# A Fourier-mixing and squared-ReLU kernel: the first phase and the first block in another order

## The chip, the cores and the metric

The kernel runs on one core of a Trainium2 chip. Its time is the device time of one execution in microseconds (us). The engines are TensorE (PE, matrix products; PEld is its weight load), VectorE (DVE), ScalarE (ACT), GpSimd (POOL), and SyncE (SP), whose queue here issues nearly all transfers.

## The reference

For x of 8 x 3008 x 256 the reference takes a Fourier transform along the sequence and one along the features, keeps the real part, and runs a two-layer network with a squared ReLU over all 24064 rows:

```python
def _attn_ref(x):
    X = np.fft.fft(x, axis=1)
    X = np.fft.fft(X, axis=2)
    return X.real.astype(np.float32)

def _moe_ref(x, w_in, w_out):        # w_in 256 x 2048, w_out 2048 x 256
    h = x @ w_in
    r = np.maximum(h, 0.0)
    g = r * r
    return (g @ w_out).astype(np.float32)
```

## The kernel before

**What is computed where.** The transform over the features is merged into the first weights: `G1` is the cosine matrix times `w_in`, `G2` the sine matrix times `w_in` (127 rows), and `gE` holds half the alternating sum of each column of `w_in`. The transform over the sequence is made once per batch from folded input: `Pt` (cosine part, 128 features), `Qt` (sine part, 127 features) and `Et` (feature 128, repeated over the partitions), each with 1505 columns, the rows of the sequence up to its middle. The rest follows by mirror symmetry: a product with `Pt` and one with `Qt`, once added and once subtracted, give the rows on both sides.

**The weights arrive as 64-bit floats** and are turned into 32-bit ones on the chip by `convert` (L213 on): a raw tile is fetched by two transfers (L227); VectorE cuts out exponent (L234) and mantissa (L239); ScalarE does three operations (L236, L237, L241); `finish` then does three on VectorE (L244, L246, L247). Raw tiles take turns in four buffers, three of which are also the buffers of x. `load_win(j)` converts one eighth of `w_in` and returns `finish` and `products`, which computes this eighth of `G1`, `G2` (L262, copied by ScalarE at L263) and `gE` (L268, L270). `load_wout(j)` converts one eighth of `w_out`.

**First phase (first batch, L711 to L747).** x comes in seven tiles (384 to 512 KB each). Tiles 0 to 3 hold the even rows of the folded sequence, tiles 4 to 6 (from `ODD0`) the odd ones. `for_p(t)` folds a tile for the cosine part (L356, L372, L386), `for_q(t)` for the sine part (L360, L376, L386). Thirty `groups` then make `Pt` (0 to 9), `Et` (10 to 19) and `Qt` (20 to 29), five for each parity of the output: products over tiles 0 to 3 (`even_n`), two joins, products over tiles 4 to 6 (`odd_n`), the last join (`join_1`, L468 to L472), which writes `Pt`, `Et` or `Qt`. The tables `cosT` and `sinT` are loaded by 13 transfers each (L182): ten small ones for tiles 0 to 3 and three large ones for tiles 4 to 6. All of x is issued ahead of both tables; the first eighth of `w_in` ahead of all.

**Main loop (L767).** A batch has six blocks of about 251 columns and each block eight steps `j`. In a step, `front` multiplies 2 x 128 columns of the hidden layer (PE L551 and L552), and VectorE forms the sums (L554, L556, L557); `combine` squares on ScalarE (L566, L567) and, outside the first block, prepares sums on POOL for a scheme with seven products instead of eight; `back`, two steps later, multiplies by `w_out`: L591 in the first block, L604 elsewhere. In the first block (steps 0 to 7) the other eighths of the weights are converted and multiplied between `back` and the next `front` (L796 to L798). In the second block `sum_wout` forms combinations of `w_out` (L282 to L285). Folding and transform of the next batch are "side work": `between`, called twice a step, takes pieces from a list by their estimated times. For the second batch it starts in the second block at half pace.

**What sets the order.** Nothing is rescheduled: each engine carries out its instructions in the order in which the code issues them. The PSUM buffers are: two for `front` (psh, tag h), two for the transform and `gE` (psd, tag d), and four accumulators mA to mD (psm). The order of issue is therefore the schedule, and a wait on one engine holds everything behind it on this engine.

The lines of the first phase and of the loop that the change replaces are printed here.

Of the kernel before, what the change touches and what calls it, by code (L numbers as in the profile page):

```python
# [13 lines left out]
P = 128  # L14
# [67 lines left out]
def kernel(  # L82
# [78 lines left out]
    sind = const.tile([P, 2, P - 1], F32, name="sind")  # L161
    altd = const.tile([P, 2, 1], F32, name="altd")
# [6 lines left out]
    G2 = const.tile([P - 1, F], F32, name="G2")  # L169
    gE = const.tile([P, NFC], F32, name="gE")  # L170

    def load_table(tab, src, engine):

        for t, (c, r0, step, rows) in enumerate(TILES):
            for i, (s0, count) in enumerate(row_tiles(S)):
                mine = [r for r in range(count) if (s0 + r - r0) % step == 0 and 0 <= (s0 + r - r0) // step < rows]
                if mine:
                    o, m = (s0 + mine[0] - r0) // step, len(mine)
                    while m % 15 and m % 16 and o + m < P and mine[0] + step * m < P:
                        m += 1  # L180
                    nk = NC[0][c]
                    engine.dma_start(out=tab[o:o + m, :, PLACE[t]:PLACE[t] + nk],  # L182
                                     in_=src[mine[0]:mine[0] + step * (m - 1) + 1:step, :, i, 0:nk])
# [5 lines left out]
    for dst, src in ((cosd, cos_d), (sind, sin_d), (altd, alt_d)):  # L189
        nc.scalar.dma_start(out=dst, in_=src.rearrange("(c p) m -> p c m", p=P))  # L190

# [61 lines left out]
    def load_win(j):  # L253
# [4 lines left out]
        def products():  # L258
            for tab, G, n in ((cosd, G1, P), (sind, G2, P - 1)):
                ps = psh.tile([P, CH], F32, name="pg", tag="h")  # L260
                for i in range(2):
                    nc.tensor.matmul(ps[0:n], tab[:, i], w[:, i], start=i == 0, stop=i == 1)  # L262
                nc.scalar.copy(G.rearrange("p (h j f) -> j p h f", h=2, j=NJ)[j],  # L263
                               ps[0:n].rearrange("p (h f) -> p h f", h=2))
            ps = psd.tile([P, CH], F32, name="pe", tag="d")
            for h in range(2):
                for i in range(2):
                    nc.tensor.matmul(ps[:, h:h + 1], w[:, i, h * P:(h + 1) * P], altd[:, i],  # L268
                                     start=i == 0, stop=i == 1)
            nc.scalar.mul(gE[:, j::NJ], ps[:, 0:2], 0.5)  # L270

        return finish, products

    def load_wout(j):

        return convert(wout[:, j].rearrange("p h c e -> p h (c e)"), pair_out(j)), lambda: None
# [158 lines left out]
    def dft_ops(b):  # L435
# [7 lines left out]
        def group(kp, which):  # L443
# [40 lines left out]
            def odd_n():  # L484
                ps = psd.tile([P, 512], F32, name="pd", tag="d")[0:n]
# [55 lines left out]
    def front(b, k0, n, j, between):  # L541
# [4 lines left out]
        for h in range(2):  # L546
# [5 lines left out]
            nc.tensor.matmul(hQ, G2[:, fs], qt[:, ks], start=True, stop=True)  # L552
# [29 lines left out]
    def back(n, j, g, s, final):  # L582

        if j == 0:
            for nm in ("mA", "mB", "mC", "mD"):
                acc[nm] = psm.tile([P, 2, CH], F32, name=nm, tag=nm)
# [20 lines left out]
    def gather(n, plain, final):  # L607


        mA, mB, mC, mD = (acc[nm] for nm in ("mA", "mB", "mC", "mD"))  # L610
        if plain:
# [3 lines left out]
            return c  # L615
        sA = ep.tile([P, 2, CK], F32, name="sA", tag="sA")
# [64 lines left out]


    weights = [lambda j=j: load_win(j) for j in range(2)]
    for j in range(NJ):
        weights.append(lambda j=j: load_wout(j))
        if j + 2 < NJ:
            weights.append(lambda j=j: load_win(j + 2))

    def next_weight():

        nonlocal begun
        (finish, products), begun = begun, weights.pop(0)() if weights else None
        finish()
        return products

# [15 lines left out]
    begun = weights.pop(0)()  # L711
    for t in range(NT):
        load_x(0, t)
    load_table(cosT, cos_s, nc.sync)
    load_table(sinT, sin_s, nc.sync)
    start()
    for_p(0)
    finish, products = begun
    finish()
    products()  # L720
    for t in range(1, 4):
        for_p(t)
    groups_at(0, 5)
    for_p(4)
    for_q(0)
    for_q(1)
    groups_at(1, 2)
    for_p(5)
    groups_at(6, 7)
    for_p(6)  # L730
    groups_at(3)
    for_q(4)
    groups_at(4, 8)
    for_q(5)
    groups_at(9, 10)
    for_q(6)
    groups_at(11, 12, 13)
    begun = weights.pop(0)()
    groups_at(15)
    for_q(2)  # L740
    groups_at(14, 16, 17, 18)
    for_q(3)
    groups_at(20, 19, 25)
    products = [next_weight()]
    groups_at(21, 22, 23, 26, 27, 28)
    next_weight()
    groups_at(24, 29)  # L747
# [6 lines left out]
    def between():  # L754
# [3 lines left out]
        if i < NJ or i % NJ == LAG - 1:  # L758
            return
        spent -= pace / 2 if i < 2 * NJ else pace  # L760
        while side and spent <= 0:
            t, f = side.pop(0)
            f()
            spent += t

    flight, finished = [], []
    for i in range(len(steps) + LAG + 4):  # L767
        if i < len(steps):
# [8 lines left out]
            if i % per == 0:  # L777
                assert not side
                side = ahead(b + 1) if b + 1 < B else []
                calls = 2 * (NJ - 1) * len(BLOCKS) - 6  # L780
                spent, pace = 0.0, sum(t for t, _ in side) / (calls - (0 if i else 3 * (NJ - 1)))
            g = front(b, k0, n, j, between)
            if i < NJ:
                s = combine(n, g, True)
            elif i < 2 * NJ:
                sum_wout(j)
# [9 lines left out]
        for f in products:  # L796
            f()
        products = [next_weight() for _ in range(2 if 0 < i < NJ - 2 else 1 if i < NJ else 0)]  # L798
# [65 lines left out]
```

## Time and profile before

| what | value |
|---|---|
| median of 3 runs | 1963.36 us (1962.3 to 1965.45) |
| the profiled execution | 1965.78 us, span of its instructions 1964.0 us |
| PE busy | 1929.5 us (98% of the span) |
| PEld, DVE, ACT, POOL busy | 1708.3, 1399.8, 924.9, 1170.2 us |
| chain that ended last | PE 93%, DVE 3%, DMA 1%, ACT 1% |
| mean granted PE clock | 0.992 |

The page cuts the span into 40 slices of 49 us. PE is at 9 tenths in all but the first (5 tenths, granted clock 7 tenths) and the last. In the first slice the DMA engines are busy 6 tenths of the time and move 186 GB/s, later 11 to 55. So the first 100 to 130 us differ from the rest, and answers about single stretches, lines and waits are needed for them. A row of such an answer names a line, an engine, an operation and its tiles; "[0.74 <-ACT ...]" says that the engine was idle for 0.74 us ahead of it and that ACT ended that wait.

### The profile page before, as it was taken

To read this page: it belongs to the slowest core of one execution; us is meant where nothing else is said; L and a number is where in the kernel's file an instruction comes from. 1 tells how busy PE (TensorE), PEld (TensorE's weight loads), DVE (VectorE), ACT (ScalarE), POOL (GpSimd) and SP (SyncE) were. 2 spreads that over 40 slices of the span, in tenths; PEclk is the share of its full clock that TensorE was granted. 3 is DMA by queue.
4 is the path that set the end of the run, shared out by engine and by line. 5 is a ranking of instruction groups with operands and counts; after the bars stand their busy time and mean duration, and the time that the engine had idled before them with its cause. 6 is when DMAs were issued, how large, how long until landed. Compare 5 with 4: busy or idle time off the path is not lost.

```text
span 1964.0 us, 27513 instructions
## 1 busy us (share of the span) xinstructions
PE 1929.5 (98%) x9160; PEld 1708.3 (87%) x9160; DVE 1399.8 (71%) x3434; ACT 924.9 (47%) x1076; POOL 1170.2 (60%) x1705
## 2 busy tenths in 40 slices
PE   5999999999999999999999999999999999999998
PEld 4788888888988889888988889888898888988887
DVE  7889866777677776777667776677767777656554
ACT  1654544445344544444444454444544454444443
POOL 0026745667566765666557765666756676556564
PEclk7999999999999999999999999999999999999999
DMA  6332101210121111111011200121002101100101
GB/s 186 113 50 52 27 13 39 50 27 20 16 51 41 21 29 27 40 30 38 11 35 33 48 19 11 35 54 27 19 15 53 33 11 22 27 11 11 22 11 22
DMA packets 145340, 68.88 MB, mean 35 GB/s; under 512 B 129003, under 2 KB 136110, under 8 KB 145197
## 3 DMA queue, kind: packets, MB, share of 16 engines
q1 hardware_dynamic: 144121, 66.60, 15.4%
q8 instruction: 72, 1.18, 0.2%
q10 hardware_dynamic: 1076, 0.52, 0.1%
q14 instruction: 71, 0.58, 0.1%
HBM read 42.39 MB, written 24.68 MB: 34 GB/s over the span
## 4 chain that ended last, share of the span: by engine, by line
PE 93%; DVE 3%; DMA 1%; ACT 1%; issue 0%; SPq 0%; DVEq 0%; ACTq 0%
PE ph L552 16%; PE ph L551 16%; PE mC L604 16%; PE mA L604 16%; PE mB L604 16%; PE mD L604 8%; PE pd L455 3%; PE pd L500 2%; DMA xt<-in_x_dram 1%; DVE he L554 1%; DMA raw<-in_moe_w_in_dram 1%; DVE g L557 0%; DVE g L556 0%; ACT g L566 0%; ACT g L567 0%; DMA cosT<-in_cos_s_dram 0%
## 5 line engine op out<-in xcount | busy, mean ns | idle before, releaser
L566 ACT ACTIVATE g<-g 128x1004 f32<-128x1004 f32 (+1 forms) x384 | 399.5, 1040 | 818.7 <-DVE g L557 421.3
L574 POOL TENSOR_TENSOR s<-g 128x251 f32<-128x251 f32 (+1 forms) x376 | 246.1, 655 | 718.9 <-ACT g L567 657.5
L554 DVE SCALAR_TENSOR_TENSOR he<-Et,gE,ph 128x251 f32<-128x251 f32 (+1 forms) x768 | 361.8, 471 | 421.5 <-PE ph L552 420.4
L551 PE MATMUL ph<-Pt,G 128*128 128x251 f32 (+1 forms) x1536 | 451.8, 375 | 4.2 <-ACT G L263 3.4
L552 PE MATMUL ph<-Qt,G 127*128 127x251 f32 (+1 forms) x1536 | 451.4, 374 | 0.2 <-DVE Qt L468 0.2
L567 ACT ACTIVATE g<-g 128x1004 f32<-128x1004 f32 (+1 forms) x384 | 399.2, 1040 | 12.2
L604 PE MATMUL mC<-s,wsum 128*128 128x251 f32 (+1 forms) x1504 | 381.4, 374 | 0.0
L604 PE MATMUL mA<-g,wout 128*128 128x251 f32 (+1 forms) x1504 | 379.8, 374 | 0.0
L556 DVE TENSOR_TENSOR g<-he,ph 128x251 f32<-128x251 f32 (+1 forms) x768 | 320.5, 417 | 54.4 <-POOL s L574 0.5
L551 PEld LDWEIGHTS ph<-Pt,G 128*128 128x128 f32 x1536 | 287.2, 189 | 42.2 <-ACT G L263 4.0
L552 PEld LDWEIGHTS ph<-Qt,G 127*128 127x128 f32 x1536 | 291.2, 190 | 36.4 <-DVE Qt L468 0.6
L604 PEld LDWEIGHTS mC<-s,wsum 128*128 128x128 f32 x1504 | 285.5, 190 | 34.6
L557 DVE TENSOR_TENSOR g<-he,ph 128x251 f32<-128x251 f32 (+1 forms) x768 | 314.2, 409 | 0.0
L604 PEld LDWEIGHTS mA<-g,wout 128*128 128x128 f32 x1504 | 282.8, 189 | 34.7 <-issue 0.6
L575 POOL TENSOR_TENSOR s<-s,g 128x251 f32<-128x251 f32 (+1 forms) x376 | 283.3, 754 | 29.5
L576 POOL TENSOR_TENSOR s<-g 128x251 f32<-128x251 f32 (+1 forms) x376 | 295.3, 785 | 0.0
L577 POOL TENSOR_TENSOR s<-g,s 128x251 f32<-128x251 f32 (+1 forms) x376 | 255.1, 678 | 0.0
L604 PE MATMUL mB<-g,wsum 128*128 128x251 f32 (+1 forms) x752 | 220.5, 374 | 0.0
L604 PE MATMUL mD<-s,wout 128*128 128x251 f32 (+1 forms) x752 | 220.3, 374 | 0.0
L604 PE MATMUL mB<-s,wout 128*128 128x251 f32 (+1 forms) x752 | 219.9, 374 | 0.0
L604 PEld LDWEIGHTS mB<-g,wsum 128*128 128x128 f32 x752 | 142.6, 190 | 17.4
L604 PEld LDWEIGHTS mD<-s,wout 128*128 128x128 f32 x752 | 141.9, 189 | 17.7
(118 smaller groups left out, 1292.1 us busy)
## 6 DMA issues: line engine op xcount, KB each, us to landing
out_dram<-os SPq DMA_DIRECT2D x376, 56.0 KB
xt<-in_x_dram SPq DMA_DIRECT2D x32, 384.0 KB
xt<-in_x_dram SPq DMA_DIRECT2D x42, 128.0 KB
Et<-e_dram SPq DMA_DIRECT2D x7, 752.5 KB
xt<-in_x_dram SPq DMA_DIRECT2D x9, 512.0 KB
out_dram<-os SPq DMA_DIRECT2D x288, 6.8 KB
raw<-in_moe_w_in_dram SPq DMA_DIRECT2D x16, 256.0 KB
raw<-in_moe_w_out_dram SPq DMA_DIRECT2D x16, 256.0 KB
```

Source lines behind the costliest of these rows:

```text
L551: nc.tensor.matmul(hP, G1[:, fs], pt[:, ks], start=True, stop=True)
L552: nc.tensor.matmul(hQ, G2[:, fs], qt[:, ks], start=True, stop=True)
L554: nc.vector.scalar_tensor_tensor(out=t, in0=et[:, ks], scalar=gE[:, fc:fc + 1], in1=hP, op0=ALU.mult, op1=ALU.add)
L556: tt(out=g[:, h, 0, 0:n], in0=t, in1=hQ, op=ALU.add)
L557: tt(out=g[:, h, 1, 0:n][:, ::-1], in0=t, in1=hQ, op=ALU.subtract)
L566: act(v, v, AF.Relu)
L567: act(v, v, AF.Square)
L574: gt(out=s1, in0=g21, in1=g22, op=ALU.add)
L575: gt(out=s2, in0=s1, in1=g11, op=ALU.subtract)
L576: gt(out=s3, in0=g11, in1=g21, op=ALU.subtract)
L577: gt(out=s4, in0=g12, in1=s2, op=ALU.subtract)
L604: nc.tensor.matmul(acc[nm][:, i, 0:n], w, v[:, 0:n], start=j == 0 and i == 0, stop=j == NJ - 1, skip_group_check=True)
```

## The change

The changed kernel computes the same. It differs in the first phase, the first two blocks and their weights:

- The queue of transfers: x tiles 0 and 1, the first eighth of `w_in`, x tiles 2 and 3, the ten small transfers of the cosine table, x tiles 4 to 6, the three large ones, then the sine table.
- `awake(n)` issues n products of the identity with itself on PE, whose result nobody reads: 44 at the start, 2 after the first weights' products, 8, 8 and 10 later in the first phase.
- Folds and groups stand in another order, the `p` folds of tiles 4 to 6 ahead of most `q` folds; `odd_n` of the first batch uses psh instead of psd.
- The alternating vector becomes the 128th column of `sind`, so that `G2` has 128 rows. `gE` is then picked out of `G2` by two one-column products and scaled on VectorE. `pg` moves from psh to the accumulators mC and mD, which the first block no longer allocates.
- In the first block, a step issues the products of the next eighth of `w_in`, begins the conversion of an eighth of `w_out`, finishes the eighth of `w_in` for two steps on, begins the one for three steps on, and finishes that of `w_out` after `back`.
- Side work for the second batch starts in the third block, at a pace that is higher accordingly.

```diff
-    def load_table(tab, src, engine):
-        for t, (c, r0, step, rows) in enumerate(TILES):
+    def load_table(tab, src, tiles):
+        for t in tiles:
+            c, r0, step, rows = TILES[t]
...
-    for dst, src in ((cosd, cos_d), (sind, sin_d), (altd, alt_d)):
+    for dst, src in ((cosd, cos_d), (sind[:, :, 0:P - 1], sin_d), (sind[:, :, P - 1:], alt_d)):
         nc.scalar.dma_start(out=dst, in_=src.rearrange("(c p) m -> p c m", p=P))
+    filled = psm.tile([P, CH], F32, name="filled", tag="mB")
+
+    def awake(n):
+        for _ in range(n):
+            nc.tensor.matmul(filled[:, 0:P], ident, ident, start=True, stop=True)
...
         def products():
-            for tab, G, n in ((cosd, G1, P), (sind, G2, P - 1)):
-                ps = psh.tile([P, CH], F32, name="pg", tag="h")
+            for tab, G, nm in ((cosd, G1, "mC"), (sind, G2, "mD")):
+                pg = psm.tile([P, CH], F32, name="pg", tag=nm)
                 for i in range(2):
-                    nc.tensor.matmul(ps[0:n], tab[:, i], w[:, i], start=i == 0, stop=i == 1)
+                    nc.tensor.matmul(pg, tab[:, i], w[:, i], start=i == 0, stop=i == 1)
                 nc.scalar.copy(G.rearrange("p (h j f) -> j p h f", h=2, j=NJ)[j],
-                               ps[0:n].rearrange("p (h f) -> p h f", h=2))
+                               pg.rearrange("p (h f) -> p h f", h=2))
+        def for_e():
             ps = psd.tile([P, CH], F32, name="pe", tag="d")
             for h in range(2):
-                for i in range(2):
-                    nc.tensor.matmul(ps[:, h:h + 1], w[:, i, h * P:(h + 1) * P], altd[:, i],
-                                     start=i == 0, stop=i == 1)
-            nc.scalar.mul(gE[:, j::NJ], ps[:, 0:2], 0.5)
+                fc = j + NJ * h
+                nc.tensor.matmul(ps[:, h:h + 1], G2[:, fc * P:(fc + 1) * P], ident[:, P - 1:], start=True, stop=True)
+            return lambda: nc.vector.tensor_scalar_mul(gE[:, j::NJ], ps[:, 0:2], 0.5)
...
             def odd_n():
-                ps = psd.tile([P, 512], F32, name="pd", tag="d")[0:n]
+                pool, tag = (psh, "h") if b == 0 else (psd, "d")
+                ps = pool.tile([P, 512], F32, name="pd", tag=tag)[0:n]
...
+    start()
+    awake(44)
+    load_x(0, 0)
+    load_x(0, 1)
+    for_p(0)
+    for_q(0)
+    for_p(1)
+    win = [load_win(0)]
+    load_x(0, 2)
+    load_x(0, 3)
+    load_table(cosT, cos_s, range(ODD0))
+    for t in range(ODD0, NT):
+        load_x(0, t)
+    load_table(cosT, cos_s, range(ODD0, NT))
+    load_table(sinT, sin_s, range(NT))
+    for_p(2)
+    rounded(0)
+    win[0][1]()
+    awake(2)
+    for_p(3)
+    groups_at(0, 5)
+    awake(8)
+    for_p(4)
+    for_p(5)
+    for_p(6)
+    groups_at(3, 8, 1, 2)
+    for_q(4)
+    groups_at(6, 7)
+    for_q(5)
+    groups_at(10, 15, 4)
+    for_q(6)
+    groups_at(9, 13, 18, 11, 12, 16, 17)
+    for_q(1)
+    awake(8)
+    groups_at(14, 23)
+    win.append(load_win(1))
+    groups_at(19, 28)
+    copy_e = win[0][2]()
+    for_q(2)
+    for_q(3)
+    groups_at(20, 25)
+    awake(10)
+    copy_e()
+    win.append(load_win(2))
+    rounded(1)
+    groups_at(21, 22, 24, 26, 27, 29)
...
-        if i < NJ or i % NJ == LAG - 1:
+        if i < 2 * NJ or i % NJ == LAG - 1:
             return
-        spent -= pace / 2 if i < 2 * NJ else pace
+        spent -= pace
...
+    def weights():
+        if i + 1 < NJ:
+            win[i + 1][1]()
+        now = i - 1 if i < NJ - 1 else i
+        if now >= 0:
+            late.append(load_wout(now))
+        if i + 2 < NJ:
+            rounded(i + 2)
+        if i + 3 < NJ:
+            win.append(load_win(i + 3))
+        elif i == NJ - 2:
+            late.append(load_wout(i))
+
+    def leftover():
+        while late:
+            late.pop(0)()
...
-                calls = 2 * (NJ - 1) * len(BLOCKS) - 6
-                spent, pace = 0.0, sum(t for t, _ in side) / (calls - (0 if i else 3 * (NJ - 1)))
+                calls = 2 * (NJ - 1) * (len(BLOCKS) - (0 if i else 2)) - 6
+                spent, pace = 0.0, sum(t for t, _ in side) / calls
             g = front(b, k0, n, j, between)
             if i < NJ:
+                weights()
                 s = combine(n, g, True)
             elif i < 2 * NJ:
+                leftover()
                 sum_wout(j)
...
-        for f in products:
-            f()
-        products = [next_weight() for _ in range(2 if 0 < i < NJ - 2 else 1 if i < NJ else 0)]
+        if i + 1 < NJ:
+            late.append(win[i + 1][2]())
+            leftover()
```

## The prediction, made before the changed kernel was run

> **What bounds the kernel now.** I read the page first, then the chain of waits, then stages. TensorE (PE) is busy 98% of the span, so only the stretches in which it is not at its pace can pay. The stage table (columns: stage, its length, busy time of PE, weight loads, VectorE (DVE), ScalarE (ACT), POOL, then granted clock and DMA) shows where those are.
>
> ```profile
> 26.90:55.20 28.30, 23.58 (x66) 14.72 (x67) 23.30 (x62) 6.75 (x13) 0.00 (x0) 0.71 0.53 162
> 55.20:110.20 55.00, 50.24 (x249) 42.19 (x247) 48.57 (x104) 39.46 (x67) 0.00 (x0) 1.00 0.30 94
> 110.20:125.60 15.40, 15.38 (x72) 13.70 (x73) 12.81 (x32) 7.13 (x16) 2.61 (x4) 1.00 0.38 78
> ```
>
> From 110.2 us on PE runs step after step; the stepping of the first product of a step is 5.11 us in the first block and 4.675 later. Ahead of it lie 55 us of first phase and seven steps of the first block, where others set the pace. The chain of waits over the first phase:
>
> ```profile
> 6.34 12.30 DMA xt<-in_x_dram
> ...
> 19.96 0.56 SPq L182
> ...
> 20.56 6.29 DMA cosT<-in_cos_s_dram
> 26.99 2.87 PE pd L455 x4
> ...
> 32.08 5.32 DMA raw<-in_moe_w_in_dram
> ...
> 40.80 7.15 PE pd L455 x22
> ...
> 49.65 5.75 PE pd L455 x12
> ```
>
> x has landed at 18.64, the odd rows of the cosine table at 26.85, the next weights (raw) at 37.40; between them PE computes at a low clock. In stretches of 2 us (PE busy, then clock) one sees a busy PE at half clock:
>
> ```profile
> 28.00:30.00 2.00, 2.00 (x4) 0.50 0.48 113
> 34.00:36.00 2.00, 1.99 (x8) 1.00 1.06 254
> 42.00:44.00 2.00, 2.00 (x4) 0.50 0.00 0
> 50.00:52.00 2.00, 2.00 (x4) 0.50 0.56 190
> ```
>
> In the first block each step takes 8.50 us (VectorE turns from a front's sums to the next conversion, L234, at 73.68, 82.18, 90.68, 99.18). VectorE's order of time, start and duration first, shows why:
>
> ```profile
> 93.74 0.43 DVE L239 TENSOR_SCALAR m<-raw 128x512 uint32<-128x512 uint32 x1
> 94.91 0.69 DVE L244 SCALAR_TENSOR_TENSOR fd<-raw,fd 128x512 uint32<-128x512 uint32 x1 [0.74 <-ACT fd L237]
> 96.24 0.69 DVE L247 SCALAR_TENSOR_TENSOR win<-m,fd 128x512 f32<-128x512 f32 x1
> 96.85 0.47 DVE L554 SCALAR_TENSOR_TENSOR he<-Et,gE,ph 128x251 f32<-128x251 f32 x1
> 99.18 0.42 DVE L234 TENSOR_SCALAR fd<-raw 128x512 uint32<-128x512 uint32 x1
> ```
>
> A front takes 2.33 (96.85 to 99.18), one conversion 2.72 (99.18 to 101.90, with no wait inside), so a step is 2.33 + 2 x 2.72 + a wait of 0.73 for ScalarE's exponent = 8.50. VectorE bounds it.
>
> **The change, part by part.** I lay the new order out on each queue with these durations.
>
> *Transfers.* The chain and the table's moments of landing fit one rule of thumb: after the kernel's bytes up to x6 (3.9 MB) at about 250 GB/s, 1.5 us pass to the landing. In both programs, as built, a transfer also waits for the landing of the eighth before it, which is why SyncE's tables waited 5.9 us for x. New queue: x0, x1, win 0, x2, x3, ten even-row tables, x4 to x6, three odd-row tables, sine. x0 then lands near 6.1 (8.2 before), x1 7.4, win 0 9.4 (6.3), x2 11.1, x3 12.8. The eighth table waits for x3, two more follow at 0.43 each, so x4 is issued at 14.2 and the DMAs starve for about 3 us; x4, x5, x6 land at 18.7, 20.7, 22.4 (x6 18.64 before), and the 1.13 MB of odd rows at about 26 (26.85 before). That step gains nearly nothing by itself; the small tables only move ahead. Sine then lands by 34 and is used after 38; win 1 is issued near 30 instead of 31.5 and needed after 38; win 2 and win 3 now pass wout 0 on the queue, which is first read in step 1.
>
> *VectorE to the first front.* p0 and q0 (1.59 each) from 6.1 to 9.3, p1 10.9, win 0 begun 11.6, p2 13.2, win 0 finished 15.1, p3 16.7, then it waits for x4 to x6: p6 ends at 24.0. Left after that: joins of six groups, 6 x (0.98 + 0.92) = 11.4; q of six tiles, 6 x 1.58 = 9.5; conversions, 0.67 + 0.67 + 2.05 = 3.4; one gE: 24.4 us, all but the last half join ahead of the first Q product. Without a wait the first Q product starts at 47.9; it started at 56.02.
>
> *TensorE to the first front.* At 0.425 us for 251 columns (the stepping above) a 377-column product is 0.64: six odd groups 6 x 1.92 = 11.5, four even ones 4 x 0.96 = 3.8, and 18 awake products at 0.22 = 3.9: 19.2 us from 26.0 on. That fits beside the 24 us of VectorE only at full clock. The 44 products at the start lie under the wait for x and weights (44 x 0.22 = 9.5, at half clock 19; even that ends at 20, and the next PE work that matters waits till 26): nothing. The eight after the even groups end near 21, and PE idles to about 24 to 26. The row: before, a cold PE went back to full clock after 5.9 us of work (begun at 26.99), 5.7 (at 40.80) and 3.7 (at 49.65), as the share of each 2 us stretch in which the clock is 1.00 gives it. The Trainium skill, "TensorE: Matmul & The Clock Gate", section "What's actually happening", says that one idle window of about 3.4 us throttles and one busy one releases. It speaks against the change here: the gap after those eight is about as long as that window. By the rule a cold start costs 3.4/2 = 1.7 us, by the rows' mean 5.1/2 = 2.6. I take the rows: PE ends its odd P groups near 32.4, VectorE then waits for its products at several joins, and the schedule's first Q product comes at 50.1, so **5.9 us** earlier (8.1 with a warm clock).
>
> *gE.* The removed alternating products cost PE 0.95 a step; two 1-column products replace them. The copy moves from ACT (0.19) to VectorE, where no such row exists: between 0.06 (its smallest memset) and 0.19; I take 0.15, 1 us in the block. Two waits are added. PE's product waits for ACT's copy of G2; the next front is queued behind it and needs that copy anyway. VectorE's gE waits for that product, which stands behind back's eight (3.4 us) on PE, and the next front's sums are queued behind gE: PE is through by 3.9 us after a front's end, VectorE gets there at 5.4, so 1.5 us cover it. sind's 128th column and G2's 128th row change no duration (pg 1.13, copy 0.37). The odd groups' move to the other PSUM pair (psh) and pg's to mC, mD cost nothing: each is read before its next use, except that odd groups wait for the join two before, which the schedule holds.
>
> *First block.* Each step now begins the next conversion before it finishes an older one, so the 0.73 wait is covered: after a front come 0.67, a finish of 2.05, 0.67, and only then, 3.4 us on, the finish that needs ACT's row from the start of the step (G copies 0.65 and 1.4 for the exponent). Steps: 5.2, four of 7.9 (2.33 + 2 x 2.72 + 0.15), 7.2, 8.3 (two wout in one), against 6.1, five of 8.5 and 6.1. One more conversion lies in the loop than before (13.7 against 13). In the old order PE's step 7 waited for the G copies behind ACT's squares, to 110.22; now G copies come ahead of them. PE's step 8 started at 115.42 = 59.4 after the first Q product; now it waits for VectorE's front 7 at 54.1 after it: **5.3 us** more. ACT needs 0.65 + 4 + 2.1 = 6.8 of 7.9, PE 7.1; both stay covered, by 1.1 and 0.8.
>
> *Later.* Side work for the second batch leaves block 1: the stalls there (L604's first product at 127.34 and seven steps on at 161.48: 34.14 instead of 32.73, so 1.4 us) go. Its pace in blocks 2 to 5 rises by 57/50 calls. Between 176 and 220 VectorE was busy 39.8 of 44 us, 4.23 a step, of which folds are 1.66; times 1.14 gives 4.46 of 4.675. I take 1.4 us of new stalls (between 0 and 3), which cancels those.
>
> **Sum**: 5.9 + 5.3 + 0 = 11.2 us, off the profiled span of 1964.0 (run 1965.78, so 1.8 lies around it and stays). The median was 1963.36; 1963.4 - 11.2 = **1952.2**.
>
> **Rivals.** (1) *The clock stays as before.* For: it was 0.71 over 26.9 to 55.2 although PE was busy 23.6 of 28.3. Against: the awake products fill the gaps. Then 19.2/0.71 = 27, first Q at 26 + 27 + 2 = 55; gain 1 + 5.3: 1957. (2) *The step does not shrink*: another wait (ACT's G copies, weights landing late) takes the 0.73's place. Against: covers of about 1 us, and 7.6 us between a buffer's release and its need, where a raw pair took 5.3 to land. Gain 5.9: 1957.5. (3) *The reorder does not bring the first phase forward*: odd rows later than 26 by as much as x4 to x6 are later (3.8), 29.8 instead of 26; gain 5.9 - 3.8 + 5.3 = 7.4: 1956. (4) *Slower: VectorE becomes the bound in blocks 2 to 5.* Folds last some 16 steps; to lose more than the 11.2 gained, a step must cost VectorE 0.7 over the 4.675, that is 5.4 instead of 4.46, folds 2.8 instead of 1.89. For: fold rows there are already stretched (L356 0.83 against 0.68 early, when POOL was idle). At 0.9 over: 1963.4 - 11.2 + 14.4 = 1966.6. (5) *Clock at half throughout*: 26 + 38.4 + 2 = 66.4, 10.4 later than before, less 5.3: 1968.5; it decides below a mean of 0.58.
>
> **Chances and numbers.** Forecast 0.62, (1) 0.15, (2) 0.09, (3) 0.06, (4) 0.04, (5) 0.04. A measurement of this kernel tells about 0.2%, 3.9 us, from no change. The forecast is faster by that throughout, (1) to (3) mostly (0.25 of 0.30), (4) and (5) are slower: faster 0.87, same 0.05, slower 0.08. The forecast's own range is 1948.5 (warm clock, no new stalls: 13.4 + 1.4 gained) to 1956; (1) to (3) extend it to 1959, and 1947 leaves room for a shorter first phase.
>
> **What would show it.** First Q product at 48 to 52 us; steps of 7.9 without a wait at the exponent's merge; PE's step 8 at 102 to 105; clock 1.00 for most of 32 to 50; PE stepping 4.675 in block 1 and nearly so up to 230. The forecast is wrong if the clock row shows 0.5 past 34, if odd rows land after 28, if steps stay at 8.5, or if PE waits for VectorE's sums in blocks 2 to 5.

## The result and the profile after

The changed kernel takes 1957.03 us (median of 6 runs, 1956.04 to 1959.73), the kernel before, on the same chip, 1964.01 us (6 runs, 1962.3 to 1966.93). The ratio is 0.9965 with a 95% interval of 0.9953 to 0.9978: faster by 7.0 us, where 11.2 were forecast. The two profiled executions have spans of 1954.8 and 1964.0 us, 9.2 apart.

Both traces are laid beside each other at four marks: the start of the first Q product of the loop (the first product of `front` with `Qt`); the first product into mA of step 10's `back` (the first one of the form used from the second block on); the same product 7 steps later; and again 17 steps later, when the folds are over. Between the first two marks lies the start of the loop, the next 7 steps are the second block less its first step, and the 17 steps hold the folds of the next batch if they were left to these blocks.

| kernel | start to first Q | to step 10 | 7 steps | 17 steps | rest of the span |
|---|---|---|---|---|---|
| before | 56.02 | 71.32 | 34.14 | 79.57 | 1722.95 |
| changed | 48.50 | 67.30 | 32.84 | 83.13 | 1723.03 |
| gain | 7.5 | 4.0 | 1.3 | -3.6 | -0.1 |

So the whole difference lies in the first 241 us, and one stage has become slower. The stages of the changed kernel (columns: stage, its length, busy time of PE, PEld, DVE, ACT and POOL, granted clock, DMA share and GB/s):

```profile
26.00:48.50 22.50, 21.26 (x109) 15.79 (x109) 21.59 (x63) 4.89 (x10) 0.00 (x0) 0.96 0.61 181
48.50:103.87 55.37, 52.74 (x242) 45.99 (x243) 52.13 (x118) 42.03 (x64) 0.00 (x0) 0.94 0.34 109
103.87:115.80 11.93, 11.93 (x57) 10.51 (x56) 11.29 (x29) 8.44 (x16) 2.73 (x4) 1.00 0.25 38
115.80:148.64 32.84, 32.84 (x155) 29.02 (x154) 28.66 (x74) 14.48 (x15) 19.28 (x28) 1.00 0.44 26
148.64:231.77 83.13, 81.25 (x375) 70.11 (x374) 74.93 (x167) 41.57 (x49) 56.10 (x79) 1.00 0.19 48
```

The same view of the kernel before for its last two stages:

```profile
127.34:161.48 34.14, 33.38 (x156) 28.82 (x155) 32.52 (x81) 14.49 (x15) 20.42 (x28) 1.00 0.42 33
161.48:241.05 79.57, 79.57 (x376) 70.59 (x375) 69.31 (x161) 42.73 (x53) 56.94 (x80) 1.00 0.18 42
```

The reader is to see three things. In the last stretch of the first phase the clock is 0.96, where before it was 0.71, and VectorE is busy 21.59 of 22.50 us. Before, PE had its gap in the second block (33.38 busy of 34.14) and none in the 17 steps; in the changed kernel it is the other way round (81.25 of 83.13). And in those 17 steps VectorE does 5.6 us more work, over 3.56 us more time.

The chain of waits over the first phase of the changed kernel (start, duration, what):

```profile
14.39 8.04 DMA xt<-in_x_dram
22.44 0.02 issue
22.46 0.70 DVE fs L366
...
24.26 11.86 PE pd L465 x40
36.12 1.79 PE filled L197 x16
37.91 3.80 PE pd L465 x12
...
47.90 0.56 DVE Qt L478
48.45 0.04 issue
48.50 0.70 PE ph L564 x2
```

The last x lands at 22.44, and from there to the first Q product no transfer ends a piece of the chain. In the kernel before the odd rows of the table, the next weights, and three PE stretches at low clock stood there. The order in time of VectorE in the first block (start and duration first; a number in brackets is the idle time ahead):

```profile
85.71 0.69 DVE L254 SCALAR_TENSOR_TENSOR wout<-m,fd 128x512 f32<-128x512 f32 x1
86.32 0.15 DVE L280 TENSOR_SCALAR gE<-pe 128x2 f32<-128x2 f32 x1
86.59 0.48 DVE L566 SCALAR_TENSOR_TENSOR he<-Et,gE,ph 128x251 f32<-128x251 f32 x1
...
88.92 0.42 DVE L241 TENSOR_SCALAR fd<-raw 128x512 uint32<-128x512 uint32 x1
...
98.01 0.69 DVE L251 SCALAR_TENSOR_TENSOR fd<-raw,fd 128x512 uint32<-128x512 uint32 x1 [0.53 <-ACT fd L244]
```

The merge that waited 0.73 to 0.76 us for ScalarE in five of the seven steps is no longer followed by a bracket, save once, at 98.01; gE is there, 0.15 long. The fronts' sums start at 49.23, 54.42, 62.35, 70.73, 78.66, 86.59, 93.72 and 102.16: steps of 5.19, 7.93, 8.38, 7.93, 7.93, 7.13 and 8.44 us, where they were 6.10, five times 8.50, and 6.09.

### The profile page after: what moved, and what is told of

Its sections match the earlier page's. It is cut to its first block, busy times and chain, and to the rows that moved or that the text cites. A ratio compares the mean times of both kernels' runs of the same rounds, so it can differ in the third digit from the quotient of the medians.

```text
span 1954.8 us, 27739 instructions
## 1 busy us (share of the span) xinstructions
PE 1935.8 (99%) x9272; PEld 1719.2 (88%) x9272; DVE 1405.2 (72%) x3442; ACT 925.3 (47%) x1068; POOL 1168.7 (60%) x1705
## 4 chain that ended last, share of the span: by engine, by line
PE 95%; DVE 3%; DMA 1%; ACT 1%; issue 0%; POOL 0%; SPq 0%; DVEq 0%; ACTq 0%
PE ph L563 16%; PE ph L564 16%; PE mC L616 16%; PE mA L616 16%; PE mB L616 16%; PE mD L616 8%; PE pd L465 3%; PE pd L512 2%; DMA xt<-in_x_dram 1%; PE mB L603 1%; PE mA L603 1%; PE pg L269 0%; DVE w L396 0%; DVE he L566 0%; DVE g L568 0%; DVE g L569 0%
```

## The experiments

All are edits of the changed kernel except one. The stage table of each is at the end of this section and comes from one profiled execution of each. The times are medians, with "before" measured on the same chip; e1 to e4 ran on one chip, e5 to e8 on a second, e9 to e11 on a third and e12 on a fourth, so medians of different chips are compared by their distance from "before". PE is called cold where the clock row shows 0.50, half clock, and warm where it shows 1.00.

**The changed kernel once more (e1).** No edit; a second profiled execution tells which stages repeat.

> The changed kernel once more, on the chip of the next three, as their yardstick. Both theories: 7 to 9 us faster than before, span near 1955, first Q product (L564) at 48.5, step 10's first product of back (L616) 11.5 us earlier than before, of which 9.3 are left after the folds of the second batch (by 230 us).

1957.64 us against 1964.72, ratio 0.9966 (0.9954 to 0.9979). The last three stages repeat to 0.01 us, the loop's start to 0.4. The first Q product moved from 48.50 to 49.90. In stretches of 2 us the first execution shows a cold PE only till about 28 us:

```profile
24.00:26.00 2.00, 1.74 (x3) 0.71 (x4) 1.93 (x7) 0.00 (x0) 0.00 (x0) 0.59 0.56 95
28.00:30.00 2.00, 2.00 (x8) 1.16 (x7) 1.93 (x6) 0.00 (x0) 0.00 (x0) 1.00 0.64 130
```

and the second till past 30:

```profile
24.00:26.00 2.00, 1.79 (x3) 0.73 (x4) 1.93 (x7) 0.00 (x0) 0.00 (x0) 0.50 0.77 150
28.00:30.00 2.00, 2.00 (x5) 1.13 (x4) 1.93 (x6) 0.00 (x0) 0.00 (x0) 0.50 0.61 116
30.00:32.00 2.00, 2.00 (x10) 1.33 (x10) 1.93 (x6) 0.00 (x0) 0.00 (x0) 0.87 1.00 349
```

So the same code has a warm and a cold start. Over all kernels here that keep this first phase, the clock over 24 to 30 us goes with the first Q product: 1.00 with 48.30 (e4 below), 0.72 with 48.50 (the changed kernel) and 48.73 (e11), 0.50 to 0.59 with 49.90, 50.35 and 50.62 (e1, e3, e2). In the trace's own record of the clock that is no cold stretch, one of 3.41 us (24.34 to 27.75 and 25.67 to 29.08), and one of 6.83 us (23.70 to 30.53 in e1).

**Even rows of the cosine table after all of x (e6).** This is undone alone:

```diff
-    load_table(cosT, cos_s, range(ODD0))
     for t in range(ODD0, NT):
         load_x(0, t)
-    load_table(cosT, cos_s, range(ODD0, NT))
+    load_table(cosT, cos_s, range(NT))
```

> The changed kernel with the ten even-row transfers of the cosine table behind x4 to x6 again, as before. Theory A (the order gains nearly nothing by itself: x6 lands 3 us earlier, but the odd rows still land near 26.5 and the groups of P wait for them): first Q product within 1 us of 48.5. Theory B (the even rows ahead of the last x make the gain of the first phase): 3 us or more later.

1957.72 us against 1964.04, ratio 0.9967 (0.9954 to 0.998). VectorE gets the last x 1.8 us earlier, at 20.67 instead of 22.46, but waits just behind it for an even group's product (its order of time; the second row's bracket is the wait):

```profile
20.67 0.69 DVE L366 TENSOR_TENSOR fs<-xt 120x512 f32<-120x512 f32 x1
...
23.97 0.25 DVE L478 TENSOR_TENSOR db<-da,pd 128x95 f32<-128x95 f32 x1 [1.61 <-ACT da L473]
```

The first Q product comes at 50.93, with a clock of 0.50 up to 28 us. That is 2.4 from the 48.5 to which both theories refer, so neither's number is met; but it is only 0.6 later than the mean of the three executions above with the same 6.83 us at half clock (50.3), which themselves lie 0.7 apart. What the table's place gives is what x's delay takes: by these single profiles this part of the change is worth less than 1 us by itself.

**No idle products (e5).** All five calls of `awake` are taken out; nothing reads their product.

```diff
-    awake(44)
...
-    awake(2)
...
-    awake(8)
...
-    awake(8)
...
-    awake(10)
```

> The changed kernel without any of the 72 idle products. Theory A (from 22.4 us, the landing of x6, VectorE bounds the first phase, with TensorE just under it): without them the clock falls to 0.5 in more of 14 to 48, TensorE's 15.3 us of products take over 20, and the first Q product comes 1 to 3 us later (49.5 to 51.5). Theory B (the idle products carry the gain of the first phase): 5 us or more later, near 54. Theory C (they do nothing): within 0.5 us of 48.5.

1957.64 us against 1964.04, ratio 0.9966 (0.9953 to 0.9979). The first Q product came at 48.01, no later than with them (Theory C's number), although the clock was 0.50 from 23 to 30 us. From there to step 10 it took 69.25 instead of 66.9 to 67.3:

```profile
44.00:46.00 2.00, 0.00 (x0) 0.00 (x0) 1.93 (x7) 1.89 (x3) 0.00 (x0) 1.00 0.37 115
46.00:48.00 2.00, 0.69 (x2) 0.30 (x2) 1.93 (x7) 0.00 (x0) 0.00 (x0) 0.81 0.42 147
48.00:50.00 2.00, 1.99 (x5) 1.66 (x6) 1.13 (x3) 0.00 (x0) 0.00 (x0) 0.50 0.00 0
52.00:54.00 2.00, 2.00 (x6) 1.31 (x4) 1.97 (x4) 0.37 (x1) 0.00 (x0) 0.50 0.00 0
54.00:56.00 2.00, 1.54 (x9) 1.23 (x9) 0.95 (x4) 1.69 (x4) 0.00 (x0) 0.99 0.72 237
```

PE ran out of work at 43.7, was cold when the loop began, and VectorE, at 1.13 busy of 2, waited for it. In the changed kernel the clock is 1.00 from 28 to 58. The idle products thus pay about 2 us at the loop's start and, in the one execution seen, nothing ahead of it. The other side of this: PE has to carry them out, and when it is cold they stand in front of groups' products. Added up, the mark in step 10 comes at 117.26 us here and at 115.39 to 117.75 in the six executions with the changed kernel's first phase, and the median is 6.4 us below before's, as it is 7.0 and 7.1 below in the changed kernel's two measurements. A gain from the 72 idle products as a whole is not shown.

e5 and e6 also leave something over. The first phase's gain is neither in the table's place nor in the idle products, so by these two runs it lies mainly in what is left: the order of folds and groups, the first weights behind two tiles of x, and the other PSUM pair. No run took these apart.

**The loop's part alone (e7).** The first phase in the order of before, without idle products, with the loop of the changed kernel.

```diff
-    start()
-    awake(44)
-    load_x(0, 0)
... (the first phase of the changed kernel)
+    win = [load_win(0)]
+    for t in range(NT):
+        load_x(0, t)
+    load_table(cosT, cos_s, range(NT))
+    load_table(sinT, sin_s, range(NT))
... (the groups in the order of before, odd_n in psd)
```

> The first phase in the order of before, without idle products, with the changed kernel's first block and its side work. Theory A (two separate gains): first Q product at 53.5 to 55 (one conversion fewer ahead of it), and from there to step 10's back 67 to 68 us, about 4 us less than before; span about 4 us shorter than before's, 1959 to 1961. Theory B (the first block's gain comes from what the new first phase leaves ready): no gain in the loop, span 1962 to 1965.

1965.14 us against 1964.04, ratio 1.0005 (0.9996 to 1.0015): no gain in time. The stages say why. The first Q product came at 57.31; in this first phase VectorE waits 5.41 us, up to 17.38, for gE's product on PE, with the folds of x behind that wait, so the edit is not before's first phase to the letter.

```profile
17.38 0.16 DVE L280 TENSOR_SCALAR gE<-pe 128x2 f32<-128x2 f32 x1 [5.41 <-PE pe L278]
```

The loop's start took 67.27, 4.05 less than before's 71.32, and the 17 steps 82.59, 3.0 more. So the loop's gain does not need the new first phase, and the loss in the folds doesn't come from it.

**Ten idle products in step 1 (e3).** In the changed kernel PE waits 2.17 us in step 1 for the copy of `G`, and the clock record shows half clock from 58.48 to 65.30 (order of time of PE):

```profile
58.58 1.01 PE L278 MATMUL pe<-ident,G 128*128 128x1 f32 x4 [2.17 <-ACT G L270]
59.45 1.19 PE L563 MATMUL ph<-Pt,G 128*128 128x251 f32 x2
```

```diff
             win[i + 1][1]()
+            if i == 1:
+                awake(10)
         now = i - 1 if i < NJ - 1 else i
```

> Adds ten idle products of the identity to step 1, behind the products of the third eighth of w_in, where TensorE waited 2.2 us for ScalarE and then ran at half clock from 58.5 to 65. Theory A (that cold stretch put TensorE 2.9 us behind, which it keeps as its bound at 7.27 us a step up to step 8): clock 1.00 there, step 8's first product about 1.3 us earlier (102.6 instead of 103.9), span 1 to 1.5 us shorter. Theory B (VectorE bounds these steps, the cold stretch is hidden): step 8 within 0.3 us, span the same.

1958.0 us against 1964.72, ratio 0.9967 (0.9955 to 0.998). The loop's start took 66.86, against 66.90 to 67.30 without. Theory A wanted step 8 1.3 us earlier; behind the first Q product it came 0.7 earlier than in the changed kernel (54.65 for 55.37) and as in e1 (54.69). So up to step 10 this cold stretch costs at most 0.4 us, nearer to Theory B. In e1, where it lasted 3.41 us instead of 6.83, it cost 0.04, and e2, in which the same wait of 2.16 us was not followed by half clock at all, took 67.13. It fits that VectorE sets the step there: PE's slow products lie beside its 5.4 us of conversions.

**Side work as before (e2).** Only the start and pace of the side work are undone: from the second block on, at half pace there.

```diff
-        if i < 2 * NJ or i % NJ == LAG - 1:
+        if i < NJ or i % NJ == LAG - 1:
...
-        spent -= pace
+        spent -= pace / 2 if i < 2 * NJ else pace
...
-                calls = 2 * (NJ - 1) * (len(BLOCKS) - (0 if i else 2)) - 6
-                spent, pace = 0.0, sum(t for t, _ in side) / calls
+                calls = 2 * (NJ - 1) * len(BLOCKS) - 6
+                spent, pace = 0.0, sum(t for t, _ in side) / (calls - (0 if i else 3 * (NJ - 1)))
```

> Undoes one part: side work for the second batch starts in the second block at half pace again, at the old pace after it. Theory A (the later start is what costs the 3.6 us between step 17 and the end of the folds): the stalls of blocks 2 to 5 shrink from 3.6 to under 0.5, those of block 1 come back with 1.3, so the span is about 2 us shorter than the changed kernel's, 1952.5 to 1953. Theory B (the stalls come from where the folds fall against POOL and the stores, whatever the pace): span within 1 us of the changed kernel's.

1956.15 us against 1964.72, ratio 0.9959 (0.9946 to 0.9971). The 7 steps took 34.17 and the 17 steps 79.57, which are before's numbers: 1.33 back, 3.56 won, as Theory A has it. The span of 1954.4 instead of 1952.5 to 1953 comes from the first Q product, at 50.62.

**The kernel before with the late side work (e8).** The same lines in the other direction, in the kernel before.

```diff
-        if i < NJ or i % NJ == LAG - 1:
+        if i < 2 * NJ or i % NJ == LAG - 1:
... (and the two lines on the pace)
```

> The kernel before with one part of the change alone: side work for the second batch starts in the third block, at the higher pace. Theory A: block 1 gains 1.3 us, blocks 2 to 5 lose about 3.6, so 2 to 2.5 us longer than before. Theory B (the pace is harmless, the stalls belong to the changed kernel's other timing): same or 1.3 us shorter.

1965.88 us against 1964.04, ratio 1.0013 (1.0003 to 1.0022): slower, by 1.8 us. 32.84 and 83.12 stand in the two stages, as in the changed kernel. With e2 this shows the term from both sides: -1.3 in the second block, +3.55 in the steps behind it, **2.25 us net loss**, whatever stands ahead.

**Both edits together (e4)**: e2's and e3's lines.

> Both of the former together. If the two costs are separate, they add: about 3.3 us under the changed kernel, span near 1951.5, some 10.5 us faster than before in the medians. If the earlier block 1 only meets denser side work, less than the sum.

1953.9 us against 1964.72, ratio 0.995 (0.9938 to 0.9963). 34.18 and 79.57 again, and the first Q product at 48.30 with a clock of 1.00 over 24 to 30. The ten products of step 1 come after that, so they can't be the reason for the warm start; its loop start of 67.09 shows no gain of theirs either. PE's order of time ahead of the odd groups shows the reason. In the changed kernel:

```profile
18.73 1.95 PE L197 MATMUL filled<-ident 128*128 128x128 f32 x16
24.26 6.97 PE L465 MATMUL pd<-cosT,w 128*128 128x377 f32 x20 [3.58 <-DVE w L396]
```

and in e4:

```profile
15.57 2.07 PE L269 MATMUL pg<-win,cosd 128*128 128x256 f32 x4 [2.28 <-DVE win L254]
17.44 1.75 PE L269 MATMUL pg<-win,sind 128*128 128x256 f32 x4
...
21.65 1.95 PE L197 MATMUL filled<-ident 128*128 128x128 f32 x16
23.85 0.87 PE L465 MATMUL pd<-cosT,w 128*128 128x377 f32 x2 [0.25 <-DVE sc L382]
```

The eight idle products (two records each) end at 20.68 in the one and leave PE idle for 3.58 us. In e4 PE happened to be cold earlier (15.48 to 18.90 in the clock record), the weights' products started 1.3 us later and took 3.8 us instead of 2.2, the idle products came 2.9 later and ended right ahead of the odd groups: no gap, a warm clock. In e1, e2, e3 and e11 the gap in this place is 2.59, 2.58, 1.66 and 1.96 us, and all four show 0.50 behind it. The median of e4 is 2.25 us below e2's on the same chip, about what the first Q product came earlier in the profiled execution (2.32); that the other four executions were warm for the same reason was not seen.

**More idle products ahead of the last x (e9).** e2's lines, and

```diff
     groups_at(0, 5)
-    awake(8)
+    awake(24)
```

> The side work as before (as in the run with side work early), and the eight idle products behind the even groups of P made 24, to cover TensorE's wait of 2.6 to 3.6 us for x6 and the odd rows. Theory A (the first Q product comes at 48.3 where the clock is 1.00 between 24 and 30 us, and at 50 to 50.6 where it is 0.5 to 0.6, so the cold stretch behind the gap is what scatters it): clock 1.00 in 24 to 30, first Q at 48.0 to 48.6, span near 1952.5. Theory B (the landing of x and the tables scatters it): first Q anywhere from 48 to 51, whatever the clock.

1954.07 us (1953.56 to 1954.98) against 1963.94, ratio 0.9952 (0.994 to 0.9965). The idle products now last to the odd groups, with no wait left:

```profile
19.13 5.52 PE L197 MATMUL filled<-ident 128*128 128x128 f32 x48
24.49 1.43 PE L465 MATMUL pd<-cosT,w 128*128 128x377 f32 x4
```

The clock over 24 to 30 was 1.00 and the first Q product came at 48.12, as Theory A has it, 2.5 us earlier than in e2, which differs by these 16 products. e10 and e12, with the same 24, have 1.00 and 47.72 and 47.66. So the gap ahead of the odd groups is what made the start cold, and eight products were too few to fill it. The medians show less of it: e9's is 9.9 us below before on its chip and e2's 8.6 on its own, and the two intervals overlap.

**The sine pieces spaced (e11).** One of the stalls in the 17 steps of the changed kernel reads as follows in VectorE's order of time:

```profile
211.98 0.41 DVE L569 TENSOR_TENSOR g<-he,ph 128x251 f32<-128x251 f32 x1
213.79 1.44 DVE L440 SCALAR_TENSOR_TENSOR w<-w,turn,f 128x256 f32<-128x256 f32 x2 [1.40 <-ACT f L426]
```

and in PE's:

```profile
216.44 0.69 PE L563 MATMUL ph<-Pt,G 128*128 128x251 f32 x2 [1.08 <-DVE g L569]
```

A fold piece of VectorE (L440) waits 1.40 us for ScalarE's piece (L426), then takes 1.44; the next front's sums stand behind both on VectorE, so PE waits 1.08 for them, and that step takes 6.03 instead of 4.67. In e11 the list's time for ScalarE's piece is raised, so that the two fall in different calls; as the pace is the list's sum over the calls, every piece behind also moves a little:

```diff
-        return ops + [(0.8, f_turn), (1.3, f_even), (0.2, f_sine), (1.4, f_odd)]
+        return ops + [(0.8, f_turn), (1.3, f_even), (1.2, f_sine), (1.4, f_odd)]
```

> The changed kernel with one number: the estimated time of the side piece that multiplies by the sines on ScalarE is 1.2 instead of 0.2, so the piece on VectorE that needs its result comes at a later call. Theory A (of the 3.6 us lost in blocks 2 to 5, the largest stall, a step of 6.03 instead of 4.67, is VectorE waiting 1.4 us for those ScalarE operations, which stand behind the squares): that step falls under 5.0, and the later 17 steps take about 82 instead of 83.1 us. Theory B (plain overload of VectorE): the stall moves elsewhere, 83.1 stays or grows, since the pace rises by about 3%.

1955.03 us against 1963.94, ratio 0.9956 (0.9942 to 0.997). The 17 steps took 82.07, 1.06 less, as Theory A said, and the wait for L426 is gone. But the step that was to fall under 5.0 did not: one of 6.02 remains, now with VectorE busy through it, and PE waits as long as ahead of the edit:

```profile
210.84 0.69 PE L563 MATMUL ph<-Pt,G 128*128 128x251 f32 x2 [1.08 <-DVE g L569]
```

So the wait for ScalarE is not shown to be what the 6.03 us step needs, and the 1.06 us came from the smaller stalls, of which six steps of 4.86 to 5.24 in the changed kernel became three of 4.79 to 5.26.

**Side work in the second block at quarter pace (e10).** e9's filling, and

```diff
-        spent -= pace
+        spent -= pace / 4 if i < 2 * NJ else pace
```

with the start in the second block and the pace that follows from it (the sum over calls less 3.5 x 7).

> As the former, but side work in the second block at a quarter of the pace, and later blocks at the pace between the two. Theory A (a stall arises where VectorE's backlog behind a side piece passes its slack, so a load between the two gives stalls between them or less): block 1 loses under 0.8 of the 1.3 us, blocks 2 to 5 under 1.5 of the 3.6; span equal to the former's within 1 us. Theory B (stalls grow only past a density that the third block on reaches at the full later pace): both nearly gone, 1 us shorter than the former.

1957.39 us (1954.21 to 1958.79) against 1963.94, ratio 0.9969 (0.9956 to 0.9981). In the profiled execution, its fastest, both stages are without a stall, 32.75 and 79.44. In the second block the pace is lower than in e2, behind it between e2's and the changed kernel's; that both stalls go is nearer to Theory B, but the span is not shorter than e9's (1952.4 and 1951.8). A new wait stands behind them (PE's order of time):

```profile
229.29 0.59 PE L616 MATMUL mD<-s,wout 128*128 128x251 f32 x2
234.50 1.14 PE L465 MATMUL pd<-cosT,we 95*7 95x95 f32 x8 [2.65 <-DVE we L346]
```

A transform product was issued right behind the VectorE piece that it reads (L346), and PE waited. The other five executions were at 1957.05 to 1958.79.

**The same with that piece spaced (e12).**

```diff
-        return (folds + [start] + [(1.5, fold_columns)] + dft_ops(None) + tables
+        return (folds + [start] + [(2.7, fold_columns)] + dft_ops(None) + tables
```

> Quarter-pace side work in block 1 and the 24 idle products, as in the kernel before it, but fold_columns' list entry is 2.7 instead of 1.5, so that its product is issued about half a call later after the pieces that VectorE needs first. Theory A (the 2.7 us wait of PE was the product placed right behind the VectorE piece that it reads, and the fill keeps the clock warm): that wait goes; first Q product at 47.7 to 48.5 us, from it to the first mA product of step 10 67, block 1's seven steps and the 17 after them together 112.1 to 112.5, rest 1722.9 to 1723.1; span 1950 to 1951, median 1951.5 to 1952.5. Rival B (where pieces fall together is what matters, and the 1.2 us more in the list shift all pieces behind it): the wait moves or new ones of 1 to 3.5 us appear in the 17 steps or in the rest; span 1952 to 1954, median 1953.5 to 1956. Rival C (the kernel before it was slow in most executions because of the mean clock and not of a wait): median 1956 or above though the profiled span is 1950 to 1952.

1952.71 us (1952.55 to 1953.43) against 1963.93, ratio **0.9945** (0.9932 to 0.9959). The wait is gone, the same product has no bracket:

```profile
232.88 1.14 PE L465 MATMUL pd<-cosT,we 95*7 95x95 f32 x8
```

and the rest is 1722.79. But the pieces behind it moved, and two steps of 5.45 and 5.29 came up among the 17, which took 80.83. So A is right about the wait and the start, B about the steps; C is wrong for this kernel, whose five executions lie within 0.9 us. For e10 it is not refuted: the mean clock of its five slower executions was 0.996 to 0.997, that of the profiled one 0.998. Where they ran cold, and why, stays open: only the fast one was profiled.

| kernel | start to first Q | to step 10 | 7 steps | 17 steps | rest |
|---|---|---|---|---|---|
| e1 changed again | 49.90 | 66.90 | 32.84 | 83.12 | 1723.04 |
| e2 side work as before | 50.62 | 67.13 | 34.17 | 79.57 | 1722.91 |
| e3 ten products in step 1 | 50.35 | 66.86 | 32.84 | 83.11 | 1723.04 |
| e4 = e2 + e3 | 48.30 | 67.09 | 34.18 | 79.57 | 1722.96 |
| e5 no idle products | 48.01 | 69.25 | 32.84 | 83.12 | 1723.08 |
| e6 table after x | 50.93 | 66.89 | 32.84 | 83.11 | 1723.03 |
| e7 loop alone | 57.31 | 67.27 | 32.84 | 82.59 | 1722.89 |
| e8 before, side work late | 54.80 | 71.33 | 32.84 | 83.12 | 1722.9 |
| e9 = e2 + fill | 48.12 | 67.07 | 34.17 | 79.57 | 1722.87 |
| e10 quarter pace + fill | 47.72 | 66.83 | 32.75 | 79.44 | 1725.66 |
| e11 sine spaced | 48.73 | 66.85 | 32.84 | 82.07 | 1722.8 |
| e12 = e10, spaced | 47.66 | 66.87 | 32.75 | 80.83 | 1722.79 |

## Why the prediction came out as it did

The direction was right and 1957.03 lies in the range, 4.8 us above the forecast; the own range of the likeliest case ended at 1956, and the wider one also held three rivals, so that lying in it says little on the mechanism. Of its signs, the first Q product (48.50), the steps of 7.93 and PE's step 8 at 103.87 came as said. The one on PE stepping nearly 4.675 up to 230 failed, and a sign of being wrong came true: PE waits for VectorE's sums in blocks 2 to 5 (81.25 busy of 83.13). Two terms of the sum were too good; the first fits on the mean, in part by luck.

**First phase: 5.9 predicted, about 6.0 on the mean.** The profiled pair differs by 7.5, but the first Q product scatters. Six executions with this first phase (changed, e1 to e4, e11) have a mean of 49.40; two with before's (before, e8) have 55.41. The working holds in its parts. Its warm case of 47.9 is met by 48.30 (e4), its cold one of 50.1 by 49.90, 50.35 and 50.62. That the mean fits is luck: the forecast set a cold start against the slower of before's two, and three of the six were not cold, or cold for 3.41 us alone. The trace row and the Trainium skill ("TensorE: Matmul & The Clock Gate", "What's actually happening") gave 2.6 and 1.7 us for a cold start; with 6.83 us at half clock (50.3) less warm (48.1 to 48.3) it is 2.0 to 2.2, between both, and with 3.41 us (48.50 and 48.73) only 0.2 to 0.6. The rule's warning that the gap behind the eight products would throttle PE came true in every execution that had the gap, already at 1.66 to 2.6 us of it (e1, e2, e3, e11), where the page needs an idle window of about 3.4: here a stretch of 3.41 us in which PE was busy for less than about half was enough (last section). The forecast took this case, as the rows had it. What was off is without effect: the last x landed at 22.44 as forecast (22.4), but tiles 4 and 5 were folded at 16.93 and 19.09, 1.7 before their forecast landing, and the odd rows of the table, placed at 26, were in use by PE at 24.26. VectorE's own work then decided, as the working said: it has no wait over 0.25 us from 22.46 to 48.

**First block: 5.3 predicted, 4.0 measured (4.0 to 4.5 over all kernels with this loop except e5, whose loop began cold).** The mechanism held: the wait of 0.73 is covered, gE costs 0.15, five of the seven steps are within 0.07 of their forecast. The step that failed is the end: PE's step 8 was to start 54.1 us after the first Q product and starts 55.37 after it (48.50 to 103.87). Half of the 1.3 are steps that are longer, 8.38 for 7.9 (0.57 of waiting for PE, which had been cold) and 8.44 for 8.3. That wait is absent in e1, e2, e3, e9 and e12, and in these step 8 starts 54.65 to 54.69 after the first Q product. The other half, 0.6, stays in all of them and is PE's own: in step 7 eight products of `back` follow the front to 103.87, so step 8 can't follow VectorE's front as closely as the sum had it. In the changed kernel they run without a pause; in the others they first wait 0.56 to 0.59 for an eighth of `w_out` (VectorE's L254).

**Later: 0 predicted, a loss of 2.25 measured.** This is the mis-sized term. The forecast took 1.4 us of new stalls in blocks 2 to 5, "between 0 and 3", against 1.4 won in block 1. The 1.4 won measured 1.3; the new stalls measured 3.56, beyond the bound. The reasoning was by mean load: 4.46 of VectorE's 4.675 a step. The mean was about right (74.93 in 17 steps, 4.41 a step) and did not tell the stalls: e10 puts a part of the same pieces into the second block and has none in either, and e11 takes 1.06 off by spacing the pieces otherwise. In the two stalls that were read (changed kernel and e11), side pieces of VectorE stand directly ahead of a front's sums; one of them waits for ScalarE, the other does not. What each of the smaller stalls is made of was not read.

Of the rivals, the half clock throughout and the unchanged clock are refuted by the clock row (0.96 over 26 to 48.5), the step that doesn't shrink by 7.93, the late first phase by 22.44 and 24.26. The slower rival, VectorE as the bound in blocks 2 to 5, is right in its place and wrong in its size, 3.6 us instead of 14.4, and in its mechanism: it wanted a mean of over 4.675 us of VectorE a step, and the stalls came at 4.41.

The sum of the measured terms is 6.0 + 4.0 - 2.3 = 7.7, beside 7.0 in the medians. Read the other way, a few lines turn the result into a better kernel: with the side work partly in the second block, one piece spaced, and 16 more idle products, e12 is at 1952.71, 11.2 under the kernel before on its chip, and faster than both.

## What to carry to other kernels

Lay both traces at the same products and take the differences stage by stage: a gain of 11.5 us up to step 10 and a loss of 2.3 behind it look like one number in the median. Don't price work that is moved into free time of an engine by its mean load; look at what stands behind each piece in its engine's order: here a mean of 4.41 of 4.675 us a step went with 3.56 us of stalls, and a part of the pieces placed elsewhere with none. Count products that nobody reads as too few if they leave a gap: eight, which left 1.7 to 3.6 us open, started the next groups at half clock like none at all, and 24 did not. And measure them by the whole: with none of the 72 the median lay 6.4 us below before's, with them 7.0.

## What the runs showed of the hardware

- The clock changes on a grid. In all 14 traces every stretch of constant clock, but the last one that the trace's end cuts off, is a multiple of 3.41 us long (3.41, 6.83, 10.24, 13.65, 17.07 and so on), and the grid's place against the kernel's start differs between executions. What the clock of the next piece goes with is how busy PE was in one piece of the grid: of the pieces at full clock, all 16 with PE busy under 0.45 of the time were followed by half clock, none over 0.60, and 6 of the 16 between. (The ends of PE's products are modelled and some records are missing, so this border is rough.)
- So the length of a gap does not decide alone. The five gaps of 1.66 to 3.58 us ahead of the odd groups (changed, e1, e2, e3, e11) were followed by half clock, but the wait of 2.16 to 2.17 us ahead of step 1's gE products was in the changed kernel, where it falls into one piece, and not in e9 (nor in e2), where the grid cuts it. In the changed kernel, and then in e9 (PE busy is the first number behind the length, the clock the third from the end):

```profile
55.07:58.48 3.41, 1.34 (x7) 0.83 (x5) 3.38 (x9) 3.38 (x7) 0.00 (x0) 1.00 0.17 64
58.48:61.89 3.41, 3.31 (x10) 2.90 (x11) 3.31 (x7) 3.34 (x7) 0.00 (x0) 0.50 0.45 149
54.18:57.60 3.42, 1.85 (x9) 1.29 (x7) 3.35 (x9) 3.36 (x6) 0.00 (x0) 1.00 0.32 121
57.60:61.01 3.41, 2.82 (x15) 2.58 (x16) 3.34 (x7) 3.34 (x8) 0.00 (x0) 1.00 0.36 109
```

- The way back to full clock took one piece or two in the changed kernel and its edits: 3.41 us where PE filled the first cold piece (24.34 to 27.75 in the changed kernel, busy 3.41), 6.83 where it left a hole in it (e1, 23.71 to 27.12, busy 2.91; e5, 47.22 to 54.05). How small a hole may be stays open: busy 0.97 of the first piece was enough in e4 (15.48) and not in the changed kernel (58.48).
- Ahead of the first change that a trace records (7.28 us in the changed kernel, 31.35 in e8), its clock row shows 1.00 by default and tells nothing.
- Stages that PE or VectorE bound mostly repeated to 0.02 us between executions and kernels (32.84 in seven kernels, 83.11 to 83.13 in six of them; e7, with the same loop, had 82.59), so that a single profile of each kernel settled a term of 2.25 us, of which the medians with their intervals of 5 us could tell little.
